# Turning q and k on TensorE for the first nine pairs: twelve-token rows, one cast, q and k side by side

## The chip, the cores and the metric

One core of one Trainium2 chip. The time is the device time of one execution in microseconds (us), median over runs. "PE" is TensorE, "PEld" its weight loads, "DVE" VectorE, "ACT" ScalarE, "POOL" GpSimd, "SP" the engine that only issues DMAs here.

## What is computed

Attention for 8 batches x 8 heads over 576 tokens with a head size of 64, in two parts that are added, and then a gated feed-forward layer (FFN) on the result. The pooled part takes the mean of every 4 tokens of q, k and v, does full attention over the 144 means, and repeats each result 4 times. The local part lets each token see the tokens less than 4 away.

```python
q_d = q.reshape(B, H, Sd, factor, D).mean(axis=3)      # k_d, v_d likewise; factor 4, Sd 144
out_up = np.repeat(sm_attn(q_d, k_d, v_d), factor, axis=2)
mask = np.abs(pos[:, None] - pos[None, :]) < factor
out_local = softmax(where(mask, scale * q @ k.T, -1e9)) @ v
x = (out_up + out_local).transpose(0, 2, 1, 3).reshape(B * S, H * D)     # 4608 x 512
out = (np.maximum(x @ w_gate, 0.0) * (x @ w_val)) @ w_out                # w: 512 x 1536, 1536 x 512
```

## The kernel before

**Work.** Two heads make a pair; there are 32 pairs. A pair's q and k must stand with the 2 x 64 head dimensions in the 128 partitions (the tile `qkT`, fp16), and their means over 4 tokens in `pd`. For the first nine pairs (`N_PE = 9`) TensorE turns them; for the others a transposing DMA does (`turn_dma`), and GpSimd makes the means (`pool_q`, `pool_k`).

**Turning on TensorE.** `load_qk` puts q into `qst` and k into `kst`, 8 tokens (2 KB) of each head in each of 72 partitions, of which 80 are loaded. `cast_q` and two `cast_k` make fp16 of them in `qk16`, eight [72 x 128] blocks of q and eight of k. `turn_pe` transposes each block into PSUM (`tq_ps`, `tk_ps`), and sums four blocks at a time by matmuls against the same unit matrix (`pool_ps`), which gives the pooled q and k. A block holds the tokens u, u+8, u+16, ..., so `evict_q` (ScalarE, L263) and `evict_k` (VectorE, L266) write every eighth element of `qkT`; `evict_pooled` (L271) writes `pd`.

**Stages.** The order of instructions is written by hand. Stage s does the scores of pair s (`scores`: L340 pooled, L360 local), the softmaxes (`pooled_max` L386 and L393, `local_max` L399 and L405, `local_sub` L408 on GpSimd, `pooled_exp` L420, `local_exp` L430, weights L443 to L471), the weighted sums of pair s-2 (`pooled_out` L325, `local_out` L373) and `add_x` (L492), which writes the layer's input `xT`. It also turns pair s+1 and casts pair s+2. `turn_local` (L479) is VectorE's own transpose, `turn_pooled` (L450) a transposing DMA on SP's queue, and in stages 3 and 4 `turn_pooled_pe` does the latter on TensorE (copied out at L461). All of the attention's scores and sums share one PSUM tile `at`, so a stage's first matmuls wait until the stage before has read it, last in `add_x`.

Stages 0 to 4 are a prologue without FFN work; `ffn(3)` comes behind it. In stages 5 to 8 one or two FFN units stand between the steps (`early`), from stage 9 on four. A unit `h` is eight matmuls (L510) into two PSUM buffers `h1`, `h2`, a relu on ScalarE (L519) and a product into `gT` on VectorE (L520); a unit `y` is twelve matmuls (L525) and a copy on ScalarE (L534). FFN units and `turn_pe` take their PSUM buffers in turn from one pool of four (tag `f`).

**Loads.** SP issues all loads of q, k and v and the transposing DMAs in program order: `load_qk` runs four pairs ahead and `load_v` three. The weights are loaded by GpSimd's queue, `piece` in stages 1 to 3. The unit matrix `eye` is a 72 x 72 constant.

Of the kernel before, what the change touches and what calls it, by code (L numbers as in the profile page):

```python
# [10 lines left out]
FP32 = mybir.dt.float32  # L11
# [5 lines left out]
N_PE = 9  # L17
# [3 lines left out]
def _np_constants():  # L21

    p = np.arange(128)
    g, i = p // 32, p % 32
    j = np.arange(32)
    diff = (j[None, :] - 4) - i[:, None]
    inside = np.abs(diff) <= 3
    mask = np.zeros((128, 6, 32), np.float32)
    for n in range(6):
        key = 24 * (4 * n + g)[:, None] - 4 + j[None, :]  # L30
        ok = inside & (key >= 0) & (key < 576)
        mask[:, n, :] = np.where(ok, 0.0, NEG)
# [5 lines left out]
    return mask, p32, np.eye(72, dtype=np.float16)  # L38


def _dap(t_ap: bass.AP, extra_off: int, dims) -> bass.AP:
# [14 lines left out]
def kernel(  # L56
# [32 lines left out]
    def many(n, shape, dt, name):  # L89
        return [pool.tile(shape, dt, name=f"{name}{i}") for i in range(n)]  # L90
# [16 lines left out]
    mask = pool.tile([128, 6, 32], FP32, name="mask")  # L107
    p32 = pool.tile([128, 32], FP16, name="p32c")
    eye = pool.tile([72, 72], FP16, name="eyec")

    xT = pool.tile([128, 4, NTOK], FP16, name="xT")
    gT = many(2, [128, NJ, TCH], FP16, "gT")
# [17 lines left out]
    def load_qk(p):  # L130
        base = 2 * p * S * D
        if p < N_PE:
            for src, dst in ((q, qst), (k, kst)):
                nc.sync.dma_start(
                    dst[p % 4][0:80, :].rearrange("p (h e) -> p h e", h=2),
                    _dap(src, base, [[512, 80], [S * D, 2], [1, 512]]),
                )
            return
        nc.sync.dma_start(
            qst[p % 4][:, 0:768].rearrange("p (h j d) -> p h j d", h=2, d=D),  # L140
            _dap(q, base, [[D, 96], [S * D, 2], [96 * D, 6], [1, D]]),
        )

        st = kst[p % 4].rearrange("p (c e) -> p c e", c=4)
        base -= 256
        z = 3 if p == NP - 1 else 4
        nc.sync.dma_start(
            st[0:80, 0:z, :], _dap(k, base, [[256, 80], [72 * 256, z], [1, 256]])
        )
        if p == NP - 1:  # L150
            for lo, n in ((0, 64), (57, 16)):
                nc.sync.dma_start(
                    st[lo : lo + n, 3, :],
                    _dap(k, base + (216 + lo) * 256, [[256, n], [1, 256]]),
                )
# [39 lines left out]
        else:  # L195
            nc.gpsimd.tensor_copy(out=out, in_=in_)  # L196

    def cast_q(p, eng):
        if p < N_PE:
            copy(  # L200
                eng,
                qk16[p % 2][0:72, 0:8, :].rearrange("p u (h d) -> p u h d", d=D),
                qst[p % 4][0:72, :].rearrange("p (h u d) -> p u h d", h=2, d=D),
            )
            return
        copy(
            eng,
            qk16[p % 2][:, 0:6, :].rearrange("p j (h d) -> p j h d", d=D),
            qst[p % 4][:, 0:768].rearrange("p (h j d) -> p j h d", h=2, d=D),
        )  # L210

    def cast_k(p, c, eng):
        if p < N_PE:
            copy(
                eng,
                qk16[p % 2][0:72, 8 + 4 * c : 12 + 4 * c, :].rearrange(
                    "p u (h d) -> p u h d", d=D
                ),
                kst[p % 4][0:72, :].rearrange("p (h u d) -> p u h d", h=2, d=D)[
                    :, 4 * c : 4 * c + 4  # L220
                ],
            )
            return
        copy(
            eng,
            qk16[p % 2][0:74, 6 + 4 * c : 10 + 4 * c, :].rearrange("p r (h d) -> p r h d", d=D),
            kst[p % 4][0:74, :].rearrange("p (h c r d) -> p c r h d", h=2, c=2, d=D)[:, c],
        )

    def cast_v(p, eng):  # L230
# [5 lines left out]

    def turn_pe(p):

        x16 = qk16[p % 2][0:72]
        tq, tk = (  # L240
            fpsum.tile([128, 8, 72], FP16, name=name, tag="f") for name in ("tq_ps", "tk_ps")
        )
        for j in range(8):
            nc.tensor.transpose(tq[:, j, :], x16[:, j, :], eye)  # L244
        for j in range(8):
            nc.tensor.transpose(tk[:, j, :], x16[:, 8 + j, :], eye)  # L246
        pq = fpsum.tile([128, 4, 72], FP32, name="pool_ps", tag="f")
        for a in range(4):
            for f in range(4):
                nc.tensor.matmul(  # L250
                    out=pq[:, a, :],
                    lhsT=x16[:, 4 * a + f, :],
                    rhs=eye,
                    start=(f == 0),
                    stop=(f == 3),
                )
        return tq, tk, pq

    def flat(p):
        return qkT[p % 3].rearrange("p j t -> p (j t)")  # L260

    def evict_q(p, ps):
        nc.scalar.copy(out=flat(p)[:, 0:S].rearrange("p (i u) -> p u i", u=8), in_=ps[0])  # L263

    def evict_k(p, ps):
        nc.vector.tensor_copy(  # L266
            out=flat(p)[:, S + 4 : 2 * S + 4].rearrange("p (i u) -> p u i", u=8), in_=ps[1]
        )

    def evict_pooled(p, ps):  # L270
        nc.scalar.copy(  # L271
            out=pd[p % 3].rearrange("p t (i a) -> p t a i", a=2),
            in_=ps[2].rearrange("p (t a) i -> p t a i", t=2),
        )

    def turn_dma(p):
        nc.sync.dma_start(
            qkT[p % 3], qk16[p % 2][:, 0:14, :].rearrange("p j f -> p (j f)"), transpose=True
        )

    def pool_q(p):
# [174 lines left out]
    def turn_pooled_pe(p):  # L456
        tp = fpsum.tile([128, 8, 72], FP16, name="ad_ps", tag="f")
        ed = e_d[p % 2].rearrange("p h c (k n) j -> p (h c k) (n j)", k=2)
        for j in range(8):
            nc.tensor.transpose(tp[:, j, :], ed[0:72, j, :], eye)  # L460
        nc.scalar.copy(  # L461
            out=adT[p % 4].rearrange("p h c k g -> p (h c k) g")[:, :, 0:72], in_=tp
        )
# [117 lines left out]
    for t in vd16:  # L581
        nc.gpsimd.memset(t[64:128, 1, :], 0.0)
    for t in qk16:
        nc.gpsimd.memset(t[64:96, 6:14, :], 0.0)

    def outputs(p):
        pooled_out(p)
# [5 lines left out]
        load_w(moe_w_val, wv, lo, hi)  # L593


    cast_q(0, "act")
    cast_k(0, 0, "dve")
    cast_k(0, 1, "dve")
    cast_v(0, "pool")
    ps = turn_pe(0)  # L600
    evict_q(0, ps)
    evict_k(0, ps)
    evict_pooled(0, ps)
    cast_q(1, "act")
    cast_k(1, 0, "dve")
    cast_k(1, 1, "pool")
    for s in range(5):
        if s in (1, 2):
            turn_pooled(s - 1)
        if s < 3:  # L610
# [12 lines left out]
        local_max(s)  # L623
        local_sub(s)
        if s >= 1:
            turn_local(s - 1)
        ps = turn_pe(s + 1)
        evict_q(s + 1, ps)
        pooled_exp(s, 0)
        pooled_exp(s, 1)  # L630
        evict_vd(s, 1)
        evict_k(s + 1, ps)
        evict_pooled(s + 1, ps)
        if s >= 3:
# [34 lines left out]
    for s in range(5, NP + 2):  # L669
# [20 lines left out]
            local_max(s)  # L690
            local_sub(s)
        weights(s, 0)
        if two:
            cast_q(s + 2, "act")
        ffn(a[0])
        if now:
            pooled_exp(s, 0)
            pooled_exp(s, 1)
        if two:
            cast_k(s + 2, 0, "dve")  # L700
        if s >= 6:
            add_x(s - 2)
# [9 lines left out]
            local_weights(s)  # L712
        ffn(a[1])
        weights(s, 2)
        if two:
            cast_k(s + 2, 1, "act")
            if s + 2 >= N_PE:
                turn_dma(s + 2)
        if now:
            turn_pooled(s)  # L720
        if nxt and s + 1 < N_PE:
# [42 lines left out]
```

## Time and profile before

| | |
|---|---|
| median of 3 runs | 412.03 us (410.6 to 412.33) |
| profiled execution | 410.69 us, span 408.9 us, mean granted clock 0.979 |
| PE busy | 361.5 us (88%) |
| DVE, ACT, POOL busy | 237.6, 230.9, 188.0 us |
| DMA queue of SP | 55.09 MB, 73.2% of 16 engines' span |
| scores (L340) of stages 0 to 4 | 11.09, 17.29, 27.81, 36.65, 45.67 us |
| first FFN matmul (L510) | 55.15 us |
| scores (L340) of stages 5 to 9 | 62.02, 70.85, 81.48, 92.00, 100.05 us |

The span runs from the first to the last instruction; the execution's time has 1.8 us more around it. A line such as `L263 ACT COPY qkT<-tq_ps 128x576 ... x9 | 24.5, 2723` is a group: source line, engine, operation, what is written from what, number, then busy us in all and mean ns of one, then the engine's idle time before them with what ended it.

### The profile page before, as it was taken

To read this page: it belongs to the slowest core of one execution; us is meant where nothing else is said; L and a number is where in the kernel's file an instruction comes from. 1 tells how busy PE (TensorE), PEld (TensorE's weight loads), DVE (VectorE), ACT (ScalarE), POOL (GpSimd) and SP (SyncE) were. 2 spreads that over 40 slices of the span, in tenths; PEclk is the share of its full clock that TensorE was granted. 3 is DMA by queue.
4 is the path that set the end of the run, shared out by engine and by line. 5 is a ranking of instruction groups with operands and counts; after the bars stand their busy time and mean duration, and the time that the engine had idled before them with its cause. 6 is when DMAs were issued, how large, how long until landed. Compare 5 with 4: busy or idle time off the path is not lost.

```text
span 408.9 us, 12885 instructions
## 1 busy us (share of the span) xinstructions
PE 361.5 (88%) x5312; PEld 184.7 (45%) x5312; DVE 237.6 (58%) x445; ACT 230.9 (56%) x606; POOL 188.0 (46%) x258
## 2 busy tenths in 40 slices
PE   2635467776999999999999999999999999999996
PEld 2534334343444444444445554444444444444442
DVE  2857858775767676766666666666665332232220
ACT  4857747774566666666666566666655332322321
POOL 5555634455865566666666655556564000000000
PEclk9999999886899999999999999999999999999999
DMA  8999997999999999999999999998641200010012
GB/s 180 216 205 208 210 152 89 174 176 163 192 194 193 196 213 214 170 200 205 187 190 180 198 181 194 199 202 182 122 103 43 69 27 26 36 44 26 27 51 103
DMA packets 152362, 60.73 MB, mean 149 GB/s; under 512 B 131696, under 2 KB 144816, under 8 KB 152304
## 3 DMA queue, kind: packets, MB, share of 16 engines
q1 hardware_dynamic: 145980, 55.09, 73.2%
q0 software_dynamic: 5952, 4.72, 8.2%
q8 instruction: 41, 0.67, 0.7%
q10 hardware_dynamic: 372, 0.12, 0.2%
q14 instruction: 17, 0.14, 0.1%
HBM read 42.35 MB, written 9.44 MB: 127 GB/s over the span
## 4 chain that ended last, share of the span: by engine, by line
PE 82%; DVE 7%; ACT 7%; DMA 3%; POOL 1%; issue 1%; ACTq 0%; DVEq 0%; POOLq 0%
PE h_ps L510 46%; PE y_ps L525 23%; PE at L373 4%; PE at L360 4%; ACT qkT L263 3%; PE at L340 2%; DVE qkT L266 2%; DMA adT<-e_d 2%; PE at L310 1%; PE at L325 1%; DVE col L386 1%; DMA qst<-in_q_dram 1%; ACT qk L192 1%; DVE xT L492 1%; DVE col L405 1%; DVE sm L399 1%
## 5 line engine op out<-in xcount | busy, mean ns | idle before, releaser
L520 DVE TENSOR_TENSOR gT<-r,h_ps 128x512 f16<-128x512 f16 x108 | 73.2, 677 | 80.4 <-PE h_ps L510 60.9
L510 PE MATMUL h_ps<-xT,wg 128*128 128x512 f16 x432 | 115.9, 392 | 0.0
L510 PE MATMUL h_ps<-xT,wv 128*128 128x512 f16 x432 | 113.6, 386 | 0.0
L525 PE MATMUL y_ps<-wo,gT 128*128 128x512 f16 x432 | 98.5, 379 | 0.1
L519 ACT ACTIVATE r<-h_ps 128x512 f16<-128x512 f32 x108 | 64.4, 596 | 49.4 <-PE h_ps L510 49.4
L408 POOL TENSOR_TENSOR dd<-sm,col 128x384 f32<-128x384 f32 x32 | 26.6, 830 | 98.8 <-DVE col L405 98.7
L510 PEld LDWEIGHTS <-wv 128*128 128x128 f16 x432 | 43.2, 100 | 54.0 <-issue 5.2
L525 PEld LDWEIGHTS <-gT 128*128 128x128 f16 x432 | 42.2, 98 | 51.3 <-issue 0.4
L510 PEld LDWEIGHTS <-wg 128*128 128x128 f16 x432 | 40.6, 100 | 47.1 <-issue 4.3
L420 ACT ACTIVATE e_d<-at,col 72x144 f16<-72x144 f32 x128 | 47.7, 380 | 6.8 <-DVE sm L399 6.8
L534 ACT COPY y_sb<-y_ps 128x512 f32<-128x512 f32 x36 | 20.9, 581 | 38.7 <-PE y_ps L525 38.7
L485 ACT CAST odx<-at 128x144 f16<-128x144 f32 x32 | 8.9, 279 | 59.5 <-PE at L373 58.5
L386 DVE TENSOR_REDUCE col<-at 72x4 f32<-72x576 f32 x32 | 24.0, 750 | 31.4 <-ACT vd L434 31.3
L445 POOL TENSOR_TENSOR e_d<-e_d,col 72x576 f16<-72x576 f16 x32 | 36.6, 1144 | 11.5 <-issue 4.0
L479 DVE STREAM_TRANSPOSE pT<-pp 128x384 f16<-128x384 f16 x32 | 19.0, 595 | 29.8 <-POOL pp L471 29.8
L196 POOL CAST vw<-vst 128x768 f16<-128x768 f32 x32 | 26.4, 825 | 5.2 <-DMA vst<-in_v_dram 5.2
L192 ACT CAST qk<-qst 96x768 f16<-96x768 f32 (+1 forms) x32 | 28.7, 896 | 0.0
L471 POOL TENSOR_TENSOR pp<-ee,col 128x384 f16<-128x384 f16 x32 | 26.5, 828 | 2.8 <-DVE col L468 2.8
L310 PE MATMUL at<-vw,p32c 128*32 128x128 f16 (+1 forms) x256 | 10.0, 222 | 17.9 <-DVE xT L492 9.1
L263 ACT COPY qkT<-tq_ps 128x576 f16<-128x576 f16 x9 | 24.5, 2723 | 2.0 <-PE tq_ps L244 1.7
L194 DVE CAST qk<-kst 74x512 f16<-74x512 f32 (+1 forms) x33 | 22.1, 672 | 5.4 <-DMA kst<-in_k_dram 5.4
L266 DVE COPY qkT<-tk_ps 128x576 f16<-128x576 f16 x9 | 24.3, 2695 | 1.6 <-PE tk_ps L246 1.6
(49 smaller groups left out, 399.1 us busy)
## 6 DMA issues: line engine op xcount, KB each, us to landing
vst<-in_v_dram SPq DMA_DIRECT2D x126, 96.0 KB, 5.1
kst<-in_k_dram SPq DMA_DIRECT2D x31, 320.0 KB, 7.4
out_dram<-y_sb SPq DMA_DIRECT2D x36, 256.0 KB, 3.4
qst<-in_q_dram SPq DMA_DIRECT2D x23, 288.0 KB, 4.8
qst<-in_q_dram SPq DMA_DIRECT2D x9, 320.0 KB, 4.6
wo<-in_moe_w_out_dram POOLq DMA_DIRECT2D x12, 128.0 KB, 5.1
wg<-in_moe_w_gate_dram POOLq DMA_DIRECT2D x2, 512.0 KB, 6.9
wv<-in_moe_w_val_dram POOLq DMA_DIRECT2D x2, 512.0 KB, 8.3
```

The costliest lines, as they stand in the source:

```text
L192: nc.scalar.copy(out=out, in_=in_)
L263: nc.scalar.copy(out=flat(p)[:, 0:S].rearrange("p (i u) -> p u i", u=8), in_=ps[0])
L266: nc.vector.tensor_copy(out=flat(p)[:, S + 4 : 2 * S + 4].rearrange("p (i u) -> p u i", u=8), in_=ps[1])
L386: nc.vector.tensor_reduce(out=c[0:72, 36:40].rearrange("p (h c) -> p h c", h=2), in_=at[0:72, 0:2, SCO : SCO + 2 * SD].rearrange("p h (c j ...
L408: nc.gpsimd.tensor_tensor(out=dd[p % 2], in0=sm[p % 2], in1=_sap(col[p % 2], (0, 128), 0, [[1, 12], [0, 32]]), op=ALU.subtract,)
L420: nc.scalar.activation(out=e_d[p % 2][0:72, h, cc, 0:6, 0:24], in_=at[0:72, h, lo : lo + SD].rearrange("p (n j) -> p n j", j=24), func=AF.Exp,
L445: nc.gpsimd.tensor_tensor(out=ed, in0=ed, in1=_sap(c, (0, 72), 48, [[1, 4], [0, 6], [0, 24]]), op=ALU.mult)
L471: nc.gpsimd.tensor_tensor(out=pp[p % 2], in0=ee[p % 2], in1=_sap(col[p % 2], (0, 128), 24, [[1, 12], [0, 32]]), op=ALU.mult,)
L510: nc.tensor.matmul(out=ps, lhsT=w[:, kk, 128 * j : 128 * j + 128], rhs=xT[:, kk, TCH * c : TCH * c + TCH], start=(kk == 0), stop=(kk == 3),)
L519: nc.scalar.activation(out=r, in_=h1, func=AF.Relu)
L520: nc.vector.tensor_tensor(out=gT[c % 2][:, j, :], in0=r, in1=h2, op=ALU.mult)
L525: nc.tensor.matmul(out=ps, lhsT=gT[c % 2][:, j, 128 * t : 128 * t + 128], rhs=wo[:, j, :], start=(j == 0), stop=(j == NJ - 1),)
```

## The change

For the first nine pairs q and k share one staging tile: q in partitions 0 to 47, k in partitions 64 to 111, twelve tokens (3 KB) of each head in each. One cast instead of three makes fp16 of both; it runs on ScalarE and VectorE for pair 0, on GpSimd for pair 1 and in stages 2 to 4, and on ScalarE in stages 0, 1, 5 and 6. `turn_pe` transposes twelve [48 x 128] blocks of each, q and k alternating, each in its own half of TensorE's rows, and pools them with 24 matmuls into two PSUM buffers. The copies read PSUM across the blocks and write `qkT` in order; the pooled copy is split between ScalarE and VectorE. `eye` grows to 112 x 120 with a second unit matrix at partition 64. Three of the four staging tiles are cleared in partitions 32 to 63, and one Exp is run ahead of the first cast. For the pairs from 9 on only the name of the staging tile changes.

```diff
+    eye = np.zeros((112, 120), np.float16)
+    eye[:72, :72] = np.eye(72)
+    eye[64:, 72:] = np.eye(48)
...
-    qst = many(4, [96, 1024], FP32, "qst")
-    kst = many(4, [96, 1024], FP32, "kst")
+    st32 = many(4, [112, 1792], FP32, "st32")
...
-    qk16 = many(2, [96, 16, 128], FP16, "qk16")
+    qk16 = many(2, [112, 14, 128], FP16, "qk16")
...
         if p < N_PE:
-            for src, dst in ((q, qst), (k, kst)):
+            for src, lo, n in ((q, 0, 64 if p == 4 else 48), (k, 64, 48)):
                 nc.sync.dma_start(
-                    dst[p % 4][0:80, :].rearrange("p (h e) -> p h e", h=2),
-                    _dap(src, base, [[512, 80], [S * D, 2], [1, 512]]),
+                    st32[p % 4][lo : lo + n, 0:1536].rearrange("p (h e) -> p h e", h=2),
+                    _dap(src, base, [[768, n], [S * D, 2], [1, 768]]),
                 )
...
+    def cast_rows(p, lo, hi, eng):
         copy(
             eng,
+            qk16[p % 2][lo:hi, 0:12, :].rearrange("p u (h d) -> p u h d", d=D),
+            st32[p % 4][lo:hi, 0:1536].rearrange("p (h u d) -> p u h d", h=2, d=D),
+        )
...
-        for j in range(8):
-            nc.tensor.transpose(tq[:, j, :], x16[:, j, :], eye)
-        for j in range(8):
-            nc.tensor.transpose(tk[:, j, :], x16[:, 8 + j, :], eye)
-        pq = fpsum.tile([128, 4, 72], FP32, name="pool_ps", tag="f")
-        for a in range(4):
-            for f in range(4):
+        pq, pk = (
+            fpsum.tile([128, 3, 48], FP32, name=name, tag="f") for name in ("pq_ps", "pk_ps")
+        )
+        halves = ((0, tq, pq, eye[0:48, 0:48]), (64, tk, pk, eye[64:112, 72:120]))
+        for u in range(12):
+            for lo, turned, _, one in halves:
+                nc.tensor.transpose(
+                    turned[:, u, :], x16[lo : lo + 48, u, :], one, tile_position=(lo, 0)
+                )
+        for u in range(12):
+            for lo, _, sums, one in halves:
                 nc.tensor.matmul(
+                    out=sums[:, u // 4, :],
+                    lhsT=x16[lo : lo + 48, u, :],
+                    rhs=one,
+                    start=(u % 4 == 0),
+                    stop=(u % 4 == 3),
+                    tile_position=(lo, 0),
                 )
...
     def evict_q(p, ps):
-        nc.scalar.copy(out=flat(p)[:, 0:S].rearrange("p (i u) -> p u i", u=8), in_=ps[0])
+        nc.scalar.copy(
+            out=flat(p)[:, 0:S].rearrange("p (i u) -> p i u", u=12),
+            in_=ps[0].rearrange("p u i -> p i u"),
+        )
...
     def evict_pooled(p, ps):
+        for t, copy_ in ((0, nc.scalar.copy), (1, nc.vector.tensor_copy)):
+            copy_(
+                out=pd[p % 3][:, t, :].rearrange("p (i a) -> p i a", a=3),
+                in_=ps[2 + t].rearrange("p a i -> p i a"),
+            )
...
+    nc.vector.memset(col[0][:, 0:1], 0.0)
+    nc.scalar.activation(out=col[0][:, 1:2], in_=col[0][:, 0:1], func=AF.Exp)
+    for t in st32[1:]:
+        nc.vector.memset(t[32:64, 0:1536], 0.0)
...
-    cast_q(1, "act")
-    cast_k(1, 0, "dve")
-    cast_k(1, 1, "pool")
+    cast_rows(1, 0, 112, "pool")
     for s in range(5):
...
         cast_v(s + 1, "pool")
+        if s >= 2:
+            cast_rows(s + 2, 0, 112, "pool")
...
-        cast_k(s + 2, 0, "dve")
-        cast_k(s + 2, 1, "pool")
         pooled_weights(s)
...
         local_weights(s)
-        cast_q(s + 2, "act")
+        if s < 2:
+            cast_rows(s + 2, 0, 112, "act")
...
         weights(s, 0)
-        if two:
+        if s + 2 < N_PE:
+            cast_rows(s + 2, 0, 112, "act")
+        elif two:
             cast_q(s + 2, "act")
         ffn(a[0])
...
-        if two:
+        if two and s + 2 >= N_PE:
             cast_k(s + 2, 0, "dve")
...
-        if two:
+        if two and s + 2 >= N_PE:
             cast_k(s + 2, 1, "act")
```

`evict_k` changes as `evict_q` does, on VectorE.

More of the change, by code (lines that the diff above doesn't have):

```diff
@@ L37, in _np_constants @@
     p32[p[own], (6 * g + (i - 4) // 4)[own]] = 0.25
-    return mask, p32, np.eye(72, dtype=np.float16)
+    eye = np.zeros((112, 120), np.float16)
+    eye[:72, :72] = np.eye(72)
+    eye[64:, 72:] = np.eye(48)
+    return mask, p32, eye
 def _dap(t_ap: bass.AP, extra_off: int, dims) -> bass.AP:
@@ L108 @@
     p32 = pool.tile([128, 32], FP16, name="p32c")
-    eye = pool.tile([72, 72], FP16, name="eyec")
+    eye = pool.tile([112, 120], FP16, name="eyec")
     xT = pool.tile([128, 4, NTOK], FP16, name="xT")
@@ L139, in load_qk @@
         nc.sync.dma_start(
-            qst[p % 4][:, 0:768].rearrange("p (h j d) -> p h j d", h=2, d=D),
+            st32[p % 4][0:96, 0:768].rearrange("p (h j d) -> p h j d", h=2, d=D),
             _dap(q, base, [[D, 96], [S * D, 2], [96 * D, 6], [1, D]]),
         )
-        st = kst[p % 4].rearrange("p (c e) -> p c e", c=4)
+        st = st32[p % 4][:, 768:].rearrange("p (c e) -> p c e", c=4)
         base -= 256
@@ L196, in copy, with cast_q @@
             nc.gpsimd.tensor_copy(out=out, in_=in_)
[L198 to L205, printed above, removed]
+    def cast_rows(p, lo, hi, eng):
         copy(
             eng,
-            qk16[p % 2][:, 0:6, :].rearrange("p j (h d) -> p j h d", d=D),
-            qst[p % 4][:, 0:768].rearrange("p (h j d) -> p j h d", h=2, d=D),
+            qk16[p % 2][lo:hi, 0:12, :].rearrange("p u (h d) -> p u h d", d=D),
+            st32[p % 4][lo:hi, 0:1536].rearrange("p (h u d) -> p u h d", h=2, d=D),
+        )
+    def cast_q(p, eng):
+        copy(
+            eng,
+            qk16[p % 2][0:96, 0:6, :].rearrange("p j (h d) -> p j h d", d=D),
+            st32[p % 4][0:96, 0:768].rearrange("p (h j d) -> p j h d", h=2, d=D),
         )
     def cast_k(p, c, eng):
[L213 to L223, printed above, removed]
         copy(
@@ L226, in cast_k @@
             qk16[p % 2][0:74, 6 + 4 * c : 10 + 4 * c, :].rearrange("p r (h d) -> p r h d", d=D),
-            kst[p % 4][0:74, :].rearrange("p (h c r d) -> p c r h d", h=2, c=2, d=D)[:, c],
+            st32[p % 4][0:74, 768:].rearrange("p (h c r d) -> p c r h d", h=2, c=2, d=D)[:, c],
         )
@@ L237, in turn_pe @@
     def turn_pe(p):
-        x16 = qk16[p % 2][0:72]
+        x16 = qk16[p % 2]
         tq, tk = (
-            fpsum.tile([128, 8, 72], FP16, name=name, tag="f") for name in ("tq_ps", "tk_ps")
+            fpsum.tile([128, 12, 48], FP16, name=name, tag="f") for name in ("tq_ps", "tk_ps")
         )
-        for j in range(8):
-            nc.tensor.transpose(tq[:, j, :], x16[:, j, :], eye)
-        for j in range(8):
-            nc.tensor.transpose(tk[:, j, :], x16[:, 8 + j, :], eye)
-        pq = fpsum.tile([128, 4, 72], FP32, name="pool_ps", tag="f")
-        for a in range(4):
-            for f in range(4):
-                nc.tensor.matmul(
[L251 to L255, printed above, removed]
+        pq, pk = (
[9 more added lines that the diff above has]
+            for lo, _, sums, one in halves:
+                nc.tensor.matmul(
+                    out=sums[:, u // 4, :],
[4 more added lines that the diff above has]
+                    tile_position=(lo, 0),
                 )
-        return tq, tk, pq
+        return tq, tk, pq, pk
     def flat(p):
@@ L262, in evict_q @@
     def evict_q(p, ps):
-        nc.scalar.copy(out=flat(p)[:, 0:S].rearrange("p (i u) -> p u i", u=8), in_=ps[0])
+        nc.scalar.copy(
+            out=flat(p)[:, 0:S].rearrange("p (i u) -> p i u", u=12),
+            in_=ps[0].rearrange("p u i -> p i u"),
+        )
     def evict_k(p, ps):
         nc.vector.tensor_copy(
-            out=flat(p)[:, S + 4 : 2 * S + 4].rearrange("p (i u) -> p u i", u=8), in_=ps[1]
+            out=flat(p)[:, S + 4 : 2 * S + 4].rearrange("p (i u) -> p i u", u=12),
+            in_=ps[1].rearrange("p u i -> p i u"),
         )
     def evict_pooled(p, ps):
[L271 to L274, printed above, removed]
+        for t, copy_ in ((0, nc.scalar.copy), (1, nc.vector.tensor_copy)):
[3 more added lines that the diff above has]
+            )
     def turn_dma(p):
         nc.sync.dma_start(
-            qkT[p % 3], qk16[p % 2][:, 0:14, :].rearrange("p j f -> p (j f)"), transpose=True
+            qkT[p % 3], qk16[p % 2][0:96].rearrange("p j f -> p (j f)"), transpose=True
         )
@@ L459, in turn_pooled_pe @@
         for j in range(8):
-            nc.tensor.transpose(tp[:, j, :], ed[0:72, j, :], eye)
+            nc.tensor.transpose(tp[:, j, :], ed[0:72, j, :], eye[0:72, 0:72])
         nc.scalar.copy(
@@ L583 @@
     for t in qk16:
-        nc.gpsimd.memset(t[64:96, 6:14, :], 0.0)
+        nc.gpsimd.memset(t[64:96, 12:14, :], 0.0)
     def outputs(p):
@@ L593, in piece @@
         load_w(moe_w_val, wv, lo, hi)
-    cast_q(0, "act")
-    cast_k(0, 0, "dve")
-    cast_k(0, 1, "dve")
+    cast_rows(0, 0, 48, "act")
+    cast_rows(0, 64, 112, "dve")
     cast_v(0, "pool")
@@ L714 @@
         weights(s, 2)
-        if two:
+        if two and s + 2 >= N_PE:
             cast_k(s + 2, 1, "act")
-            if s + 2 >= N_PE:
-                turn_dma(s + 2)
+            turn_dma(s + 2)
         if now:
```

## The prediction

> **What bounds the kernel now.** I read the page's chain first. From about 55 us on it is TensorE's own work (L510, L525), which the change leaves alone; the rest is L263, L266 and a wait for a transposing DMA.
>
> ```profile
> PE 82%; DVE 7%; ACT 7%; DMA 3%; POOL 1%; issue 1%; ACTq 0%; DVEq 0%; POOLq 0%
> PE h_ps L510 46%; PE y_ps L525 23%; PE at L373 4%; PE at L360 4%; ACT qkT L263 3%; PE at L340 2%; DVE qkT L266 2%; DMA adT<-e_d 2%; PE at L310 1%; PE at L325 1%; DVE col L386 1%; DMA qst<-in_q_dram 1%; ACT qk L192 1%; DVE xT L492 1%; DVE col L405 1%; DVE sm L399 1%
> ```
>
> Next, the same chain in order of time (start us, us, what). At 21 us it hangs on the DMA that turns pair 0's pooled weights. In stage 3 (37 to 45 us) it is VectorE in its program order, and the copy-out of the turned k is the longest piece. At 67 us, after FFN units have begun, it is ScalarE's copy-out of the turned q.
>
> ```profile
> 20.97 6.44 DMA adT<-e_d
> ...
> 40.44 0.55 DVE col L405
> 41.00 0.48 DVE pT L479
> 41.48 2.59 DVE qkT L266
> 44.41 0.66 DVE xT L492
> ...
> 66.86 0.49 ACT r L519
> 67.35 0.51 ACT qk L192
> 67.86 2.63 ACT qkT L263
> ```
>
> Then the groups, shapes kept apart (count | busy us, mean ns of one). The last row moves as many elements as the first two from PSUM, and costs a quarter: it reads and writes runs of 72, the others write every eighth element (16 bytes apart).
>
> ```profile
> L263 ACT COPY qkT<-tq_ps 128x576 f16<-128x576 f16 x9 | 24.5, 2723 | 2.0 <-PE tq_ps L244 1.7
> L266 DVE COPY qkT<-tk_ps 128x576 f16<-128x576 f16 x9 | 24.3, 2695 | 1.6 <-PE tk_ps L246 1.6
> ...
> L461 ACT COPY adT<-ad_ps 128x576 f16<-128x576 f16 x2 | 1.3, 630 | 0.0
> ```
>
> **The price everything hangs on.** The new copies write in order but read PSUM at steps of 48 halves (96 bytes), which no row here does. Lower bound 0.63 us (L461) on ScalarE and 0.74 us on VectorE (L492, 576 elements from PSUM); upper bound, with nothing to exclude more, the 2.7 us of L263 and L266. Where the traced copies read PSUM out of memory order (L485, runs of 6; L492, runs of 24) they pay nothing for it: 279 ns for 144, 742 ns for 576. Those are reads, as the new step is, so I take 0.9 us, near the lower end, and keep 2.7 and beyond as rivals.
>
> **Stages 0 and 1: DMA decides.** In stages 0 and 1 compute hardly gets shorter. The casts' slopes (1024 elements 1,045 ns, 768 837 ns on ScalarE; 512 604 ns, 768 825 ns on GpSimd) give 1.5 us for the new 1536-element cast on either. PE turns with 24 + 24 instructions for 16 + 16: eight transposes take 0.41 us from start to start at the early clock and sixteen pooling matmuls 1.04, so 1.2 + 1.6 against 0.8 + 1.0 us, and q's copy starts 0.8 later because q and k alternate. That eats what a short copy-out gives here. The three memsets of 32x1536 on VectorE: the row with 64 elements took 112 ns, GpSimd's with 1024 946 ns, so 1.5 to 2.4 us each; on SP's queue the loads of pairs 1 to 3 wait for one each, the first of them issued at 6.4 us, and pair 0's k cast, behind all three on VectorE, waits until 6.1 for its data anyway. At nothing; if they are late, the next sentences hide it. The early Exp saves ScalarE the 1,283 ns table load at 4.9 us, but k's cast on VectorE (1.7 us) then ends last: nothing.
> Stage 2 starts on the 6.44 us DMA, at 27.45, and that DMA stands behind the loads of five pairs' q and k and four v's. The windows of stages 0, 1 and 2 (stretch; its length; busy us of PE, weight loads, DVE, ACT, POOL; clock; DMA share; GB/s) show the DMA engines full (packets overlap, so the share passes 1):
>
> ```profile
> 11.00:17.30 6.30, 3.40 (x94) 2.81 (x94) 5.87 (x9) 5.82 (x15) 2.88 (x4) 1.00 1.22 222
> 17.30:27.80 10.50, 3.77 (x100) 2.97 (x100) 6.97 (x13) 7.26 (x16) 7.80 (x10) 1.00 1.19 196
> 27.80:36.60 8.80, 4.18 (x152) 3.49 (x148) 6.65 (x11) 6.28 (x15) 3.35 (x4) 1.00 1.35 206
> ```
>
> Over the first 30 us they move 198 GB/s. Two 320 KB loads become two of 288 KB: 64 KB x 5 = 328 kB, 1.65 us at that rate. Bounds: 0 if row length and 48 partitions slow the queue as much, 3 us if longer rows speed it up. I take 1.6.
>
> **Stages 2 to 4: VectorE's order.** From the start of k's copy (41.41) to the start of add_x (44.33) VectorE needs 2.92 us: copy 2.30 from start to start, k cast 0.55, reciprocal 0.07. The cast leaves VectorE; half of the pooled copy comes to it (L485's 144 elements, 0.28; 0.7 at L263's price per element). New: 0.80 + 0.25 + 0.07 = 1.12, so 1.8 us less per stage, 5.4 in three. What could be late instead: ScalarE's four Exps end at 42.74 now; q's copy starts 0.75 later and is 1.8 shorter, so they end near 42, before VectorE's pooled copy. GpSimd's whole cast (1.5 for 0.6) now stands ahead of local_sub, which waits at 41.15 while GpSimd is free from 39.9: it ends at 41.4, a delay of 0.3 that add_x does not wait for. Behind it queue the weights' DMAs, 1 us later in their stage. The second turning DMA gets late: now it lands near 35 and is needed at 36.28, but the need moves ahead by 3.4 and the landing by some 2. I charge 0.6 (0 to 1.5).
>
> **Stages 5 to 7: the last FFN unit's buffers.** Four PSUM buffers of tag f are now all taken by one turn, so the pooled k sums wait for the gT product (L520) of the unit before, not only for its relu. Behind that wait on PE stand the next stage's pooled_v and scores. Stage 5: ScalarE's cast grows 0.43, the later k cast (0.61) is gone, so q's copy starts at 67.75 as before; gT ends near 68.4; 24 pooling matmuls at 34 ns (warm, sixteen took 0.55) end at 69.4, their copies at 69.7; scores at 69.75 instead of 70.85: 1.1. Stage 6, where ScalarE was not held up by the longer cast (it waited 0.48 at 74.05): relu ends at 77.7, gT 78.4, sums 79.4, scores 79.8 instead of 81.48: 1.7. Stage 7 keeps its casts: gT ends at 89.23, sums 90.2, scores 90.55 instead of 92.0: 1.45. Together 4.2. From stage 8 the rows are as before.
>
> **The sum.** 1.6 + 5.4 - 0.6 + 4.2 = 10.6 us. The profiled execution took 410.69 (span 408.9 and 1.8 around it): 400.1. The median of the runs, 412.03, lies 1.3 above it: 401.4.
>
> On eight tiles of the array 48 small matmuls take 0.56 us (L360, early clock), so q's and k's may overlap on two: three late turns 0.4 us shorter each. This 1.2 goes into the range, not into the sum. [...]
>
> **Rivals.**
> *Strided PSUM reads cost what strided writes cost (2.7).* For it: both engines show 4.7 ns per element where steps are 16 bytes, so the limit is in the memory. Against: L485 and L492. Stages 2 to 4 then gain 2.92 - 2.62 = 0.3 each; stages 5 to 7 have copies behind gT's end (68.4 + 2.7 + 0.3 and so on) and lose 0.6, gain nothing, lose 0.3. Net 1.6 + 0.9 - 0.9: 410.4, no change.
> *They cost more, and the kernel is slower.* Each microsecond of copy beyond that costs one in each of six stages, as VectorE copies k last in all of them. The gain of 1.6 is used up at 3.0 us per copy; at 4.0, 1.3 above the strided write's price, the time is 410.4 + 6 x 1.3 = 418.2. For it: nothing traced reads single elements 96 bytes apart. Against: the same as above.
> [...]
> *DMA takes the prologue's gain.* The share is 1.35, 1.21 and 1.11 in stages 2 to 4, so loads may end the next wait. Then the prologue shortens by its bytes alone, 64 KB x 8 pairs at 205 GB/s = 2.5 us; with 4.2 later, 405.3. Against: from stage 2 on no cast waits for a load.
>
> **The numbers.** Forecast 0.67; DMA 0.13; price of a strided write 0.10; dearer 0.10. A measurement of this kernel can tell about 0.5% (2.1 us) from no change. Faster: 0.67 + 0.13 = 0.80; same 0.10; slower 0.10. The forecast's own range is 397 (copies at their lower bounds 0.45, longer rows that speed the queue 1.4, no late DMA 0.6, q and k turned side by side in time 1.2, and 0.8 by which the runs lie apart) to 405 (copies of 1.3 us 1.2, loads no faster 1.6, the late DMA at its upper bound 0.9). To hold 8 in 10 it reaches over the DMA case to the price of a strided write: 397 to 410.5; the dearer case is left out.
>
> **What would show it.** L263's and L266's successors near 0.9 us: right; at 2.7: the first rival. Stage 2 starting near 25.8 and pooled_out waiting less than 1 us in stage 3: the DMA terms. Stages 2 to 4 each 1.8 us shorter, FFN starting near 48.7 instead of 55.15. Scores of stages 6 to 8 after a wait for pooled copies that ends at gT + 1.4. Wrong if GpSimd's cast or SP's queue ends the chain in stages 2 to 4, or if stages after 8 change their period of 9.45 us.

## The result and the profile after

The changed kernel takes 414.74 us (median of 13 runs, 411.2 to 415.59), the kernel before in the same session 411.92 (13 runs, 410.3 to 412.82). The ratio is 1.0066, 95% interval 1.0042 to 1.0089: slower by 0.66%, where 401.4 us and a range of 397 to 410.5 had been forecast. The profiled execution took 414.22 us with a span of 412.4, at the same granted clock (0.979) as before; span against span, 3.5 us were lost.

The copies the change was about did get cheap. The groups of the changed kernel, shapes kept apart (count | busy us, mean ns of one); L262 and L268 are the successors of L263 and L266, L465 of L461:

```profile
L268 DVE COPY qkT<-tk_ps 128x576 f16<-128x576 f16 x9 | 6.7, 742 | 3.1 <-PE tk_ps L243 3.1
...
L262 ACT COPY qkT<-tq_ps 128x576 f16<-128x576 f16 x9 | 5.7, 638 | 10.7 <-PE tk_ps L243 10.5
...
L465 ACT COPY adT<-ad_ps 128x576 f16<-128x576 f16 x2 | 1.3, 648 | 0.0
```

2723 and 2695 ns became 638 and 742, and a copy that reads PSUM every 96 bytes costs what L465 costs in memory order. So 2 us left VectorE in each stage, and yet the chain got longer. Its shares, by engine and by line:

```profile
PE 78%; DMA 8%; DVE 5%; ACT 4%; issue 3%; POOL 1%; SPq 1%; ACTq 0%; DVEq 0%; POOLq 0%
PE h_ps L514 43%; PE y_ps L529 23%; PE at L377 4%; DMA st<-in_k_dram 4%; PE at L364 4%; DMA adT<-e_d 2%; PE at L344 2%; ACT e_d L424 2%; DMA mask<-band_mask 1%; PE at L314 1%; PE at L329 1%; ACT qk L197 1%; DVE xT L496 1%; DVE gT L524 1%; D
```

Both copies are gone from the lines shown; DMA rose from 3% to 8% and "issue", time in which the engine waits for nothing the profile shows, from 1% to 3%. The same chain in order of time (start us, us, what) shows where:

```profile
10.54 8.17 DMA st<-in_k_dram
...
22.94 6.84 DMA st<-in_k_dram
...
30.27 10.10 DMA adT<-e_d
...
47.50 1.46 issue
...
51.34 4.10 issue
```

Up to 40 us, work on VectorE has been replaced by loads of q and k and by the second of the two DMAs that turn pooled weights. From 47 to 55 us TensorE stands for 5.6 us without a cause, and once more for 2.85 us at 84. The windows of stages 0, 1 and 2 (same columns as before) tell the first part:

```profile
11.20:18.20 7.00, 2.45 (x116) 1.88 (x110) 3.08 (x7) 2.88 (x13) 3.39 (x4) 1.00 1.22 170
18.20:30.80 12.60, 3.04 (x120) 2.21 (x116) 4.91 (x12) 6.25 (x16) 8.62 (x10) 1.00 1.22 182
30.80:40.80 10.00, 3.35 (x170) 2.60 (x167) 4.68 (x11) 3.38 (x14) 5.62 (x7) 1.00 1.28 171
```

VectorE's busy time falls from 5.87, 6.97 and 6.65 to 3.08, 4.91 and 4.68 us, while the stretches grow from 6.3, 10.5 and 8.8 to 7.0, 12.6 and 10.0. The DMA share stays at 1.2 to 1.3 (full), but the rate drops from 222, 196 and 206 GB/s to 170, 182 and 171: the engines are as busy and move less.

The balance, from the starts of the pooled scores (L340 before, L344 after) and the first FFN matmul:

| stretch | before | after | difference | forecast |
|---|---|---|---|---|
| start to scores of stage 2 | 27.81 | 30.81 | +3.00 | -1.6 |
| stages 2 and 3 | 17.86 | 18.59 | +0.73 | -3.0 |
| stage 4 to the first FFN matmul | 9.48 | 10.31 | +0.83 | -1.8 |
| first FFN units, to scores of stage 5 | 6.87 | 7.85 | +0.98 | 0 |
| stages 5, 6, 7 | 8.83, 10.63, 10.52 | 7.16, 8.64, 12.05 | -1.67, -1.99, +1.53 | -1.1, -1.7, -1.45 |
| rest | 316.90 | 316.99 | +0.1 | 0 |

The sum is +3.5 us, against -10.6.

### The profile page after: what moved, and what is told of

It is laid out like the page before. It is cut to its first block, busy times and chain, and to the rows that moved or that the text cites. A ratio compares the mean times of both kernels' runs of the same rounds, so it can differ in the third digit from the quotient of the medians.

```text
span 412.4 us, 13168 instructions
## 1 busy us (share of the span) xinstructions
PE 357.2 (87%) x5456; PEld 179.5 (44%) x5456; DVE 223.2 (54%) x449; ACT 210.1 (51%) x601; POOL 189.1 (46%) x256
## 4 chain that ended last, share of the span: by engine, by line
PE 78%; DMA 8%; DVE 5%; ACT 4%; issue 3%; POOL 1%; SPq 1%; ACTq 0%; DVEq 0%; POOLq 0%
PE h_ps L514 43%; PE y_ps L529 23%; PE at L377 4%; DMA st<-in_k_dram 4%; PE at L364 4%; DMA adT<-e_d 2%; PE at L344 2%; ACT e_d L424 2%; DMA mask<-band_mask 1%; PE at L314 1%; PE at L329 1%; ACT qk L197 1%; DVE xT L496 1%; DVE gT L524 1%; DVE col L390 1%
## 5 line engine op out<-in xcount | busy, mean ns | idle before, releaser
L424 ACT ACTIVATE e_d<-at,col 72x144 f16<-72x144 f32 x128 | 46.6, 371 | 9.4 <-DVE sm L403 9.3
L197 ACT CAST qk<-st 96x768 f16<-96x768 f32 (+3 forms) x51 | 40.8, 800 | 2.0 <-DMA st<-in_q_dram 1.6
L496 DVE TENSOR_TENSOR xT<-at,odx 128x576 f16<-128x576 f32 x32 | 23.9, 745 | 2.6 <-ACT odx L489 1.4
L424 ACT ACTIVATION_READ_ACCUMULATOR e_d<-at,col 72x1 f32 x128 | 25.0, 195 | 0.0
L314 PE MATMUL at<-vw,p32c 128*32 128x128 f16 (+1 forms) x256 | 10.1, 220 | 16.6 <-DVE xT L496 6.5
L329 PE MATMUL at<-adT,vd 128*32 128x144 f16 x256 | 11.3, 238 | 11.1 <-DMA adT<-e_d 9.3
```

The costliest lines, as they stand in the source:

```text
L197: nc.scalar.copy(out=out, in_=in_)
L424: nc.scalar.activation(out=e_d[p % 2][0:72, h, cc, 0:6, 0:24], in_=at[0:72, h, lo : lo + SD].rearrange("p (n j) -> p n j", j=24), func=AF.Exp,
L496: nc.vector.tensor_tensor(out=xT[:, kk, b * S : (b + 1) * S].rearrange("p (n g m f) -> p g n m f", n=6, g=4, f=4), in0=at[:, :, U : U + SD ...
```

## The experiments

Theory A: loads into 48 partitions run slower per byte. The DMA engines are full up to 55 us (the changed kernel's shares are 1.20 to 1.33 in the stretches from 11 to 55 us), so the two DMAs that turn the pooled weights of pairs 0 and 1, which SP issues behind those loads, come later, and TensorE waits for them. Theory B: DMA, by bytes or by the order on SP's queue, would hold the prologue whatever the loads look like. Theory C: TensorE's instruction stream is late in places, since a turn now has 48 matmuls and as many weight loads where it had 32. Differences in time between kernels of different sessions are taken by their ratios to the kernel before on the same chip, 1% being 4.1 us.

### The cheap copies alone

```diff
-        nc.scalar.copy(out=flat(p)[:, 0:S].rearrange("p (i u) -> p u i", u=8), in_=ps[0])
+        nc.scalar.copy(out=flat(p)[:, 0:S].rearrange("p (i u) -> p i u", u=8),
+                       in_=ps[0].rearrange("p u i -> p i u"))     # evict_k likewise
```

> The kernel before with nothing changed but evict_q and evict_k: they write in order and read PSUM at steps of 144 bytes (eight blocks of 72). Loads, casts, turns and pooled copies stay as before. Theory A (the changed kernel lost in its loads what it won in its copies): copies near 0.65 to 0.75 us, stage 2 starts at 27 to 28 us as before, stages 2 to 4 get shorter by 4 to 6 us together and stages 5 to 7 by 2 to 4, time 401 to 405 us. Theory B (the copies are no limit, whatever is won in the early stages is lost again to full DMA engines): scores of stages 3 and 4 wait for a transposing DMA and FFN starts within 1 us of 55.2, time 409 to 412 us.

406.86 us, ratio 0.9889 (0.9860 to 0.9919). The copies took 637 and 737 ns. Stage 2 starts at 27.78 (27.81 before), stage 3 at 36.87, FFN at 52.06. This lies between the two theories' numbers. Where no DMA is waited for, the forecast step is there: stage 3 shrinks from 9.02 to 7.16 us, 1.86 less (1.8 forecast). But TensorE's waits up to 60 us (engine, line, releaser: us in all, times, longest) hold two for the turning DMA, where before there was one of 3.5. The row of the kernel before, of the changed kernel and of this one:

```profile
PE at L325 <- DMA adT<-e_d: 3.5, 1, 3.5
PE at L329 <- DMA adT<-e_d: 9.3, 2, 6.2
PE at L329 <- DMA adT<-e_d: 7.7, 2, 6.0
```

So the compute of stages 0 to 2 gets shorter and the DMA takes it. Copies without any change to the loads bring 4.6 us; the change as a whole loses 2.7.

### The loads: shape against bytes

Four kernels keep the changed kernel's compute and alter only the loads of q and k. First the loads of before:

```diff
-  st32[lo:lo+48, 0:1536]  <-  [[768, 48], [S*D, 2], [1, 768]]
+  st32[0:80, lo:lo+1024]  <-  [[512, 80], [S*D, 2], [1, 512]]     # lo = 0 (q), 1024 (k)
```

> The changed kernel with the loads of before: 80 partitions, rows of 2 KB, 320 KB for q and for k of each pair, into a tile of 80 of 112 partitions by 2048; the casts still read 1536 elements of it, so the result is made from the wrong elements; everything else is as in the changed kernel. Theory A (48 partitions with rows of 3 KB slow the loads): though 64 KB more are loaded per pair, stage 2 starts at 27 to 28.5 us (30.8 in the changed kernel) and the time is 409 to 412 us. Theory B (compute or the order on SP's queue delays the transposing DMA, not the shape of the loads): stage 2 starts at 31 us or later, time 414 to 417 us.

410.87 us, ratio 0.9982 (0.9963 to 1.0001); stage 2 starts at 28.29 us. With 64 KB more per pair it is 3.5 us faster than the changed kernel. Then 48 partitions with rows of 2 KB:

```diff
-  [[768, 48], [S*D, 2], [1, 768]]
+  [[512, 48], [512*48, 3], [1, 512]]
```

> The changed kernel whose loads keep their 48 partitions and 288 KB, but in three rows of 2 KB to a partition instead of two of 3 KB; the casts then find other tokens there than they should. If the length of a row (3 KB, which the DMA engines moved at 12.6 B/ns where rows of 2 KB went at 15.3) slows the loads: q1 moves over 200 GB/s from 3 to 27 us (186 in the changed kernel), stage 2 starts at 26 to 28 us, time 408 to 411. If the 48 partitions do: rate within 5 of 186 GB/s, stage 2 at 30 to 31.5 us, time 413 to 416.

412.39 us, ratio 1.0028 (1.0007 to 1.0049); stage 2 at 30.47 us. Of the numbers expected for the partitions, the time lies just under its range and the stage start inside; the rate, 192 GB/s in the totals below, lies just above its 181 to 191. Then 64 partitions with rows of 3 KB (`n = 64` for both):

> The changed kernel whose loads fetch 64 rows of 3 KB for q and for k of each pair, 384 KB instead of 288, of which 48 are used as before. If 48 partitions slow the loads and 64 do not: over 200 GB/s from 3 to 27 us, and the third more bytes are paid at that rate: stage 2 at 31 to 33 us. If the length of a row does: the rate stays within 8 of 186 GB/s and stage 2 starts at 33 us or later, time 416 to 420.

414.25 us, ratio 1.0057 (1.0033 to 1.0080); stage 2 at 31.46 us: a third more bytes at no extra cost. And the 3 KB rows cut in two:

```diff
+  for a in (0, 384):
-      st32[...][:, :, 0:768]      <-  [[768, 48], [S*D, 2], [1, 768]]
+      st32[...][:, :, a:a+384]    <-  [[768, 48], [S*D, 2], [1, 384]]
```

> The changed kernel with every load of q or k cut into two DMAs whose rows are 1.5 KB instead of 3 KB; the partitions are the same 48. If the length of a row is what slows the loads: stage 2 starts at 28 to 29.5 us and the time is 411 to 413 us. If the number of partitions is, or bytes alone: stage 2 starts at 30.5 to 31.5 us as in the changed kernel, time 414 to 416 us.

410.29 us, ratio 0.9973 (0.9952 to 0.9994); stage 2 at 28.75 us, which is what had been expected if the length of a row were the limit, with a time a little under that range.

The DMA totals of the stretch from 3 to 27 us, for the changed kernel, old loads, 48 partitions with 2 KB, 64 with 3 KB, and 48 with 1.5 KB, in this order (under 2 KB counts all the smaller packets):

```profile
DMA packets 7773, 4.45 MB, mean 186 GB/s; under 512 B 6755, under 2 KB 6883, under 8 KB 7771
```
```profile
DMA packets 8913, 4.99 MB, mean 208 GB/s; under 512 B 7247, under 2 KB 7375, under 8 KB 8911
```
```profile
DMA packets 8491, 4.62 MB, mean 192 GB/s; under 512 B 6974, under 2 KB 7102, under 8 KB 8489
```
```profile
DMA packets 7987, 5.27 MB, mean 219 GB/s; under 512 B 6700, under 2 KB 6828, under 8 KB 7985
```
```profile
DMA packets 9130, 4.61 MB, mean 192 GB/s; under 512 B 7193, under 2 KB 9128, under 8 KB 9128
```

The kernel before moved 4.96 MB there at 207 GB/s. The trace's own list of packets up to 35 us says the same of single rows: 48 partitions go at 12.6 B/ns with 3 KB (244 ns a row), 12.5 with 2 KB (164 ns), 12.8 with 1.5 KB (120 ns); 64 partitions with 3 KB at 14.3 (215 ns); 80 partitions with 2 KB, in the kernel before, at 14.8 (138 ns, where two expectations have 134 and 15.3). So in these kernels a row's rate goes with the partitions and not with its length. It is a rate under this load: the same rows in the same 48 partitions go at 13.3 B/ns in the kernel without turning DMAs below, and at 15.7 where half of the data is loaded. Why the partitions matter was not shown. The cut rows also start stage 2 by 2 us earlier at a rate of 192, which partitions alone do not explain: the first turning DMA then lands 4.5 us after its issue at 23.9, where the changed kernel's takes 6.4 from 24.0. The packet list shows what it stands behind. In nine kernels (all with this DMA but the reordered one below) TensorE's wait for it ends 1.2 to 1.3 us after the last row of q and k that was ahead of it; at its issue 476 KB of these rows had still to land with cut rows, 675 KB in the changed kernel. Why the cut loads were further along by then was not settled.

### Taking the waits for the turning DMA away

```diff
-        if s in (1, 2):
-            turn_pooled(s - 1)
...
-        if s >= 3:
+        if s >= 1:
             turn_pooled_pe(s - 1)
```

On the kernel before with cheap copies:

> The kernel before with copies in order, and the pooled weights of pairs 0 and 1 turned by TensorE (turn_pooled_pe) instead of by a transposing DMA, as those of pairs 2 and 3 are. Theory A (what holds stages 2 and 3 is that DMA, queued behind loads in full DMA engines): its 6.0 and 1.7 us waits go, another wait, for the loads of pairs 3 and 4, takes part of them back; stage 2 starts at 22 to 25 us, time 401 to 404. If DMA bytes alone set the pace up to 55 us: FFN still starts within 1 us of 52.1 and the time is 406 to 407.5.

400.34 us, ratio 0.9714 (0.9682 to 0.9747): 7.2 us less for eight transposes and a copy in each of two stages, and 11.8 less than before. The time lies just under its range. Stage 2 starts at 24.16 us, FFN at 49.39. On the changed kernel:

> The changed kernel with the pooled weights of pairs 0 and 1 turned by TensorE instead of by a transposing DMA; loads and turns stay. Theory A, its narrow form (the slower loads cost time only through the transposing DMA that is queued behind them): the 6.2 and 3.1 us waits go and nothing takes their place, stage 2 starts at 24 to 26 us, time 402 to 405. Its wide form (loads of 48 partitions are late themselves, so casts wait for them, and TensorE's stretches without a cause stay): stage 2 at 25 to 29 us, gain of 4 to 8 us over the changed kernel, 406 to 410, still 6 or more above the kernel before with the same two edits (400.3).

403.53 us, ratio 0.9782 (0.9738 to 0.9826), 11.7 us less than the changed kernel. Stage 2 starts at 24.30, stage 3 at 31.62, within 0.2 us of the kernel with the loads of before. So the slow loads cost time through the DMA that is queued behind them, and hardly otherwise: the narrow form of theory A, except that TensorE's stretches stay, as the wide form had it. The two kernels also differ in casts and turns, so a small loss to the loads could hide behind shorter compute. The rest of that kernel's chain shows what stays:

```profile
33.09 0.15 PE tq_ps L243
34.12 4.37 issue
38.49 0.20 PE pq_ps L248
...
41.88 0.15 PE tq_ps L243
42.03 3.75 issue
45.78 0.20 PE tq_ps L243
```

8.1 us of "issue" stand inside turns. Whether the turning DMA suffers from its place or from its own length:

```diff
         if s in (1, 2):
             turn_pooled(s - 1)
-        load_v(s + 3); load_qk(s + 4)
+        if s == 1:
+            load_qk(4)          # moved here from stage 0
+        load_v(s + 3)
+        if s > 0:
+            load_qk(s + 4)
```

> The changed kernel with one thing moved: pair 4's loads of q and k stand behind the first turning DMA on SP's queue instead of ahead of it, so the same bytes go in another order. If the first turning DMA is late because its place in the queue comes after the slow loads: it is issued at 20.5 to 22 us instead of 24.0, and stage 2 starts 2 to 3 us earlier, at 28 to 29; stage 2's casts then wait for pair 4 and give part of it back: 412.5 to 414.5. If the full engines alone set its end: landing within 1 us of 30.4, time within 1 us of 414.7.

413.53 us, ratio 1.0048 (1.0021 to 1.0075), which cannot be told from the changed kernel's. The first turning DMA is issued at 21.34 instead of 24.00 and stage 2 starts at 26.09, 4.7 earlier, more than expected; but the second one, issued at 28.36, lands at 38.7, and stage 3 starts at 39.05, only 1.7 earlier. So the place in the queue moved the first, and the second, 10.3 us from issue to landing, swallows most of what was won.

### The stretches without a cause

In the changed kernel they last 1.46, 4.10 and 2.85 us up to 100 us. The DMA queues between 52.7 and 54.3 us, within the long one (packets, MB, share of 16 engines):

```profile
q0 software_dynamic: 262, 0.27, 104.7%
q1 hardware_dynamic: 122, 0.05, 14.5%
q8 instruction: 1, 0.02, 5.6%
```

The instruction queue moves one packet of 16 KB, 5.6% of 16 engines for 1.6 us, 1.4 us long. In the packet list such packets end at 47.7, 54.2 and 85.9 us, and TensorE goes on at 48.96, 55.43 and 87.26, 1.2 to 1.4 us after each. The other traces agree: up to 100 us the sixteen kernels have 42 such stretches of over 0.4 us, and each ends 1.2 to 2.0 us after a packet of this kind. Three kernels change the number of TensorE's instructions. With 6 instead of 24 pooling matmuls in a turn (`for u in range(0, 12, 4)`, each with start and stop):

> The changed kernel with 6 instead of 24 pooling matmuls in a turn, one for each group of four tokens, so the pooled sums lack three of four tokens; 18 fewer matmuls and weight loads in a turn, nothing else changed. Theory C (TensorE's instruction stream is late: 24 + 24 instructions with their weight loads for 16 + 16, fetched through full DMA engines): the stretches of 1.5, 4.1 and 2.9 us near 47, 51 and 84 us in which TensorE waits for nothing that the profile shows go, and the time falls by 5 to 8 us to 406 to 409. Theory A without C: the stretches stay within 2 us in sum, the time falls by 0 to 2 us to 412.5 to 414.5.

408.93 us, ratio 0.9924 (0.9897 to 0.9950), 5.9 us less than the changed kernel; 4.0 us of the stretches stay instead of 8.4. The same edit where the turning DMA is no longer in the way:

> The changed kernel with pooled weights turned by TensorE (403.5 us) and 6 instead of 24 pooling matmuls in a turn, so the pooled sums lack three of four tokens. If the number of TensorE's instructions makes the stretches without a cause: they fall from 11.5 us in all to under 4, time 396 to 400. If not: 9 us or more stay, time 402 to 403.5.

400.97 us, ratio 0.9738 (0.9700 to 0.9776), 1.8 us less by the ratios, whose intervals overlap, and 1 above the expected range; but TensorE's "issue" waits up to 100 us fall from 11.5 to 3.0. Of these 8.5 us little reached the time; other waits took their place. First the kernel it came from, then this one:

```profile
PE pq_ps L248 <- issue: 4.4, 1, 4.4
PE tq_ps L243 <- issue: 3.8, 1, 3.8
PE at L377 <- issue: 2.6, 1, 2.6
PE h_ps L514 <- issue: 0.7, 1, 0.7
```
```profile
PE at L377 <- issue: 1.6, 2, 1.2
PE h_ps L514 <- issue: 1.4, 1, 1.4
```

And the other way, each pooling matmul twice in the kernel with cheap copies:

> The kernel before with copies in order (406.9 us) and each pooling matmul issued twice, so the pooled sums are double: 16 more matmuls and weight loads in a turn, as many instructions as the changed kernel has in a turn; loads and copies unchanged. If TensorE's instruction count costs time because fetches come late: stretches of over 1 us without a cause in the profile appear between 40 and 56 us and the time grows by 3 to 6 us, to 410 to 413. If not: 16 matmuls more cost 0.6 to 1 us in stages 5 to 7 and hide before, time 407 to 409.

409.43 us, ratio 0.9939 (0.9916 to 0.9963), 2.1 us more; stretches of 0.80 and 3.65 us appear that end at 44 and 51 us, where the kernel it came from had none before 60. Up to 100 us it is 7.0 us of them against 5.2, for that kernel has two later ones of 2.83 and 2.34. It cost a little less than expected. Is it the full DMA engines that make the stretches? With half of the data loaded, in the changed kernel with TensorE's turns:

```diff
+  z = 2 if p in (0, 4) else 1
-  st32[...][lo:lo+n, 0:1536]    <-  [[768, n], [S*D, 2], [1, 768]]
+  st32[...][lo:lo+n, 0:768*z]   <-  [[768, n], [S*D, z], [1, 768]]
```

> The changed kernel with pooled weights turned by TensorE (403.5 us), and of seven of the first nine pairs (not 0 and 4) only the first head's half of q and k is loaded, 144 KB less for each of q and k; the other half is left at zeros. In it TensorE stood 4.4, 3.8, 0.7 and 2.6 us without a cause in the profile. If these are instruction fetches that come late because the DMA engines are full: under 3 us of them stay before 60 us, time 394 to 398. If TensorE's instruction rate alone makes them, whatever the DMA engines do: 6 us or more of them stay before 60 us, and the time gains only what the loads held, 400 to 403.

399.75 us, ratio 0.9714 (0.9678 to 0.9749), and 3.71 and 2.11 us of stretches before 60 us: 5.8 of the 8.1, between the two expectations and nearer to the second. The first of the two still fell in full engines (a share of 1.29 from 31.4 to 35.1 us) and lasted 3.71 for 4.37; the second, from 38.6 to 40.7 us, fell where the share was 0.49, and lasted 2.11 for 3.75. So the second stretch came without full engines; that they lengthen one fits this pair and is not shown by it alone.

Fewer instructions of TensorE go with shorter stretches (8.4 to 4.0 us, 11.5 to 3.0), and more of them with two new ones ahead of 60 us, but their number is not all. With the turns of before, 32 matmuls each, the kernel before has no stretch over 0.4 us up to 100 us, though ten 16 KB packets of the instruction queue fall there, the one with cheap copies has 5.2 us of them, the one with TensorE's turns too 4.2, and the one with 72 rows (below) none again. So single traces with the same turns lie up to 5 us apart, and the 1.8 us between 7.0 and 5.2 say little by themselves. That the number of instructions matters is likely by the 4.4 and 8.5 us; what else decides was not tested.

### Two more edits to the fastest kernel

Loads of 72 instead of 80 rows:

> The kernel at 400.3 us (copies in order, pooled weights turned by TensorE) whose loads of q and k of the first nine pairs fetch 72 rows instead of 80, as only 72 are used: 64 KB fewer per pair. If bytes alone count: the loads end 0.3 us earlier per pair, time 397 to 399.5. If 72 partitions move at a lower rate than 80, as 48 did: packets of 2 KB take over 145 ns instead of 134 and the time is 400 to 402.

402.22 us, ratio 0.9772 (0.9727 to 0.9817). Packets took 138 ns, 14.9 B/ns, between the expectations and as long as those of 80 rows in the kernel before; the bytes saved bring nothing that can be told. The early Exp:

> The kernel at 400.3 us with one thing more of the change: a small Exp ahead of everything, so that ScalarE loads its table before pair 0's data is there (1.28 us, at 4.82 now). ScalarE's first cast starts at 4.9 instead of 6.1. If the first stages are held by compute: stage 0 starts 0.6 to 1.2 earlier and the time is 399 to 399.8; if by the loads that stages 1 and 2 wait for: 400 to 400.8, no change that can be told.

400.99 us, ratio 0.9720 (0.9678 to 0.9763): no change, as if held by loads. Stage 0 did start 0.3 us earlier (9.64 us for 9.92). The fastest kernel stays the one with ordered copies and TensorE's turns, at 400.34 us, 11.8 below the kernel before and 14.5 below the changed one.

## Why the prediction was wrong

The forecast of -10.6 us and the measured +3.5 lie 14.1 us apart. By the table, 4.6 of them arose up to the scores of stage 2, 3.7 in stages 2 and 3, 2.6 in stage 4, 1.0 in the first FFN units and 2.1 in stages 5 to 7.

**The price everything hangs on** was right, and pessimistic: 0.64 and 0.74 us for 0.9. Both rivals about strided reads fell: copies took 638 and 742 ns at steps of 96 bytes (the changed kernel), and 637 and 737 at 144 (the cheap copies alone). What limits the writes at steps of 16 bytes, 4.7 ns per element on both engines, was not shown.

**Stages 0 and 1, "DMA decides"** is the first step that failed, and the largest. It took DMA as the bound, rightly, and then turned 64 KB less per pair into 1.65 us at 198 GB/s. The rate was held fixed while the shape of the loads changed; it fell by 10% (207 to 186 GB/s from 3 to 27 us) as the bytes did (4.96 to 4.45 MB), and with everything behind SP's queue 3 us later (the first turning DMA issued at 24.00 for 20.97), -1.6 became +3.0. The lower bound had named "48 partitions slow the queue as much" and stopped at zero, with no reason given that excluded a loss. Old loads in the changed kernel bring stage 2 to 28.29, so 2.5 of the 3.0 hang on how the data is loaded. Rows cut in two bring back 2.1 with the same 48 partitions, so the lower rate into 48 partitions is shown, but not that it alone makes the 3.0; that part of the cause stays open. A sign of being wrong that the prediction named, SP's queue ending the chain in stages 2 to 4, is what the trace shows: TensorE's last long waits ahead of the scores of stages 2 and 3 are for the turning DMAs, 6.2 and 3.1 us.

**Stages 2 to 4, "VectorE's order"**: the 1.8 us per stage were real (stage 3 with cheap copies alone: 1.86; without turning DMAs, stage 2 goes from 8.84 to 7.28). What failed next is the cover: "the second turning DMA gets late" was charged 0.6 with an upper bound of 1.5, but it is a chain piece of 10.1 us, TensorE waits 3.1 for it in stage 3, and stages 2 and 3 grew by 0.73 instead of shrinking by 3. The rival "DMA takes the prologue's gain" had the right mechanism and the wrong price, for it also let the bytes shorten the prologue by 2.5.

**Stage 4 and after**: TensorE's turn was priced by its slope alone (1.2 + 1.6 us). What the prediction calls the early clock and warm was seen in times alone: before the change sixteen pooling matmuls took 1.16 us up to 48 us and 0.68 at 67 us, at a granted clock of 1.00 both times. Where nothing stopped it, it ran in 0.47 + 0.47 us, less than the 0.9 + 1.0 before; but 4.10 us before the FFN and 2.85 in stage 7, in which TensorE stood, were in no term; the 16 more instructions in a turn are their likely cause, and that it is they alone is not shown. Stages 5 and 6 gained 1.67 and 1.99 (1.1 and 1.7 forecast), and stage 7 without its 2.85 would have gained 1.3 (1.45 forecast). The side-by-side turn, which the prediction had in its range and not in its sum, was also right: in the turn at 14.9 us one of q and one of k start together and the next two 40 ns later, where those of before started 58 ns apart, one by one, in the turn at 12.0.

## What to carry to other kernels

A kernel whose early stages run at a DMA share above 1 (1.2 to 1.3 here) must be costed by what the new loads move per microsecond (186 GB/s here), not by bytes at the old rate (207), and the first thing to ask of a transfer that is waited for is what is queued ahead of it. When the copy that ends a stage is made four times cheaper, look at once for the next wait at the same instant (here a transposing DMA), take it away as well, and the gain appears: 4.6 us with one edit, 11.8 with two. With 18 small matmuls fewer in a turn TensorE's busy time fell by 4.9 us, the kernel's time by 5.9 and the stretches from 8.4 to 4.0, so look in the trace for time in which the engine waits for nothing.

## What the runs showed of the hardware

- In full engines (shares of 1.14 to 1.20 from 3 to 27 us) rows into 48 partitions (0 to 47 and 64 to 111) moved at 12.5 to 12.8 B/ns per engine at 1.5, 2 and 3 KB, into 64 at 14.3, into 80 at 14.8. The figure is one of the load too: rows into 48 went at 15.7 with half of the data loaded (share 1.08).
- TensorE's wait for the first transposing DMA ended 1.2 to 1.3 us after the last row of q and k ahead of it on SP's queue, in nine kernels.
- ScalarE read 128x576 halves from PSUM at steps of 96 or 144 bytes in 0.64 us, as fast as in order (0.65); VectorE took 0.74. Writes to SBUF at steps of 16 bytes took 2.7 on both.
- TensorE stood for 0.4 to 4.6 us at a time with no wait that the profile shows, and went on 1.2 to 2.0 us after a 16 KB packet on the instruction queue had ended, 42 times in sixteen traces.
- The first four FFN matmuls took 1.89 us, later ones 1.03, at a granted clock of 1.00 (kernel before). In the changed kernel the slower times lasted three groups instead of two, the 0.98 us of the table; its cause was not tested.
